# One fit of scales, accumulating x transfers from GpSimd's queue, and a new list of x work in a fused attention and gated feed-forward kernel

## Chip, cores and metric

The kernel runs on one core of one Trainium2 chip. The metric is the device time of one execution in microseconds (us). The kernel before takes 801.61 us, the median of three runs (801.25 to 802.07).

## The reference, cut to what matters

```python
def reference(**kwargs):
    attn_out = _attn_ref(**attn_kwargs)        # [4, 8, 576, 64], softmax attention with a bias of positions
    x = attn_out.transpose(0, 2, 1, 3).reshape(B * S, H * D)      # [2304, 512]
    return _moe_ref(x=x, **moe_kwargs)

def _moe_ref(x, w_gate, w_val, w_out):         # [512, 1536], [512, 1536], [1536, 512]
    gate = 1.0 / (1.0 + np.exp(-(x @ w_gate)))
    val = x @ w_val
    return (gate * val @ w_out).astype(np.float32)
```

The three weight matrices of the feed-forward arrive as float64, the rest as float32; the output is float32. The change lies in the second part, the gated feed-forward.

## The kernel before, in words

**Attention** writes its result to a DRAM tensor `xs`, in which every head has two partial rows (the products with the high and the low part of a split value matrix), and the reciprocals of the softmax sums to `rs`. So a block of x, 128 model columns by 384 tokens, is the sum of two partial blocks of `xs`, times a block of `rs`.

**The feed-forward** (`Moe.run`, line 1162) takes the 2304 tokens as six chunks of 384. Float32 numbers are split into a high and a low part, and each product is three matmuls (high by high, high by low, low by high).

*Chunks 0 and 1* run in 24 steps, numbered 0 to 23, whose order is the string `ORDER` (line 48): a step is one chunk with one of the 12 blocks of 128 hidden columns. In a step TensorE makes the 24 matmuls of gate and value (`gates`, line 890) and then the 9 output matmuls of the step before (`outs`); the last step makes no output matmuls. ScalarE and VectorE apply the sigmoid, the multiply and the split (`gated`, line 905). Beside this the steps convert the float64 weights to float32 blocks, store them to a DRAM tensor `scratch` for later, and take the sum of squares of each block on ScalarE (line 873).

*Chunks 2 to 5* run as two pairs (q = 1: chunks 2 and 3; q = 2: chunks 4 and 5). For a pair, gate (z = 0) and value (z = 1) are 2 by 2 block products with seven multiplications in place of eight (the tables `SUMS`, `VARS` and `PRODUCTS`, lines 71 to 77). Six pairs of hidden blocks by two z by two token pairs make 24 *halves*, `half(h)` (line 1050): even h are z = 0, odd h are z = 1, h = 0 to 11 the first pair, 12 to 23 the second. A half makes seven products of six matmuls in float16 parts, with some output matmuls of the halves before between them; VectorE adds PSUM banks and gates, ScalarE copies banks and applies the sigmoid. In a half, GpSimd makes four sums of weights for the half after the next (line 1036), ScalarE and VectorE make scaled float16 high and low parts of weights for the next half (lines 1042 and 1047), and SyncE's queue loads weights for the third half from here (line 1029).

**The x work of a pair** is a set of small commands, run by `x_do` (line 942), one for each of the blocks B11, B12, B22, B21 (first index: half of the model columns, second index: token chunk) and two slices kc = 0 and 1 of each:

- `l`: load the two partial blocks (`load_x`, line 797: two transfers of 64 partitions) and the reciprocals (`load_r`, two more), all on SyncE's queue;
- `+`: VectorE adds the two partial blocks into a tile `xt` (line 952);
- `*`: VectorE multiplies by the reciprocals (line 954), and ScalarE takes the sum of squares (line 956);
- `T1` to `T4`: VectorE forms the four differences of `SUMS` (line 960);
- `h` and `-`: ScalarE makes the scaled high part (line 966), VectorE the scaled low part (line 968) of each of the seven blocks of `VARS`.

These commands are written out by hand. For the first pair `XTIMES` gives, for each block, the step of `+` and `*` and the step of the load, and `XPLAN` gives the rest by step (the commands are issued at the end of that step; a letter `W` or `S` with a digit loads or sums the weights of half 0, 1 or 2, `h` and `v` with one digit make the parts of half 0's weights, `o` loads output weights). For the second pair `XFILL` is a list with `|` between entries: an entry is taken after each of the seven products of an even half and after the first and third of an odd half, from half 1 on.

**The scales** come from the squares. `fit` reduces squares to a maximum on VectorE, `norm` sums over partitions by a matmul on TensorE that stands in a step after the gates (`NORM`) or in a half after the last product, `read` takes the result out of PSUM, and `fitted` makes the powers of two with small VectorE operations. Before, there are three fits: fit 0 (x of the first pair and the weights of hidden blocks 0 to 7, "A") behind step 18, fit 1 (weights of blocks 8 to 11, "B", and the output weights) behind step 20, and fit 2 (x of the second pair) in half 6. So gate and value have two sets of scales, by hidden block, and `gs` holds two factors for the gating multiply.

**Order.** Each engine and queue runs its instructions in the order in which the program issues them. SyncE's queue holds all loads and stores of this stage; GpSimd has no transfers.

Of the kernel before, what the change touches and what calls it, by code (L numbers as in the profile page):

```python
# [715 lines left out]
class Moe:  # L716
# [212 lines left out]
    def store(self, c, t):  # L929
# [5 lines left out]
        i = 6 + c // 2 - 1  # L935
        self.nc.scalar.activation(out=ob, in_=po, func=AF.Copy, **({"scale": self.ends[:, i:i + 1]} if c > 1 else {}))
# [32 lines left out]

    def xtile(self, q):  # L970
        return self.pools["xt" if q == 1 else "xt2"].tile([128, self.T], F32, tag="xt", name="xt")

    def fit(self, b):

        s = self.squares
        for i, g in enumerate(((s[:, 24:32], s[:, 0:16]), (s[:, 16:24], s[:, 40:52]), (s[:, 32:40],))[b]):
            self.nc.vector.tensor_reduce(out=self.most[:, 2 * b + i:2 * b + i + 1], in_=g, axis=mybir.AxisListType.X, op=ALU.max)  # L980
# [178 lines left out]
    def run(self):  # L1159
# [4 lines left out]
        with ExitStack() as ph, tc.manual_schedule():  # L1164
# [111 lines left out]
```

## Time and profile before

| | us |
|---|---|
| median of three runs (lowest, highest) | 801.61 (801.25, 802.07) |
| the profiled execution, whole | 801.25 |
| its span, first to last instruction | 799.5 |
| TensorE busy in the span | 757.7 |
| VectorE busy | 665.3 |
| ScalarE busy | 572.8 |
| GpSimd busy | 344.7 |

The page names TensorE matmuls PE and weight loads PEld, VectorE DVE, ScalarE ACT, GpSimd POOL and SyncE SP; L952 is line 952 of the kernel. Times in the views are microseconds from the start of the span unless marked ns. The attention part ends at about 370 us; the steps run from 362 to 520 us and the halves from there to the end. Step 18 begins at 481.20, half 0 at 520.28, half 1 at 531.87 and half 12 at 658.25, each read off the first matmul of the step or half.

### The profile page before, as it was taken

To read this page: it belongs to the slowest core of one execution; us is meant where nothing else is said; L and a number is where in the kernel's file an instruction comes from. 1 tells how busy PE (TensorE), PEld (TensorE's weight loads), DVE (VectorE), ACT (ScalarE), POOL (GpSimd) and SP (SyncE) were. 2 spreads that over 40 slices of the span, in tenths; PEclk is the share of its full clock that TensorE was granted. 3 is DMA by queue.
4 is the path that set the end of the run, shared out by engine and by line. 5 is a ranking of instruction groups with operands and counts; after the bars stand their busy time and mean duration, and the time that the engine had idled before them with its cause. 6 is when DMAs were issued, how large, how long until landed. Compare 5 with 4: busy or idle time off the path is not lost.

```text
span 799.5 us, 17532 instructions
## 1 busy us (share of the span) xinstructions
PE 757.7 (95%) x6359; PEld 605.2 (76%) x6359; DVE 665.3 (83%) x1358; ACT 572.8 (72%) x1222; POOL 344.7 (43%) x401
## 2 busy tenths in 40 slices
PE   7999989999999999898999999988999999999997
PEld 4888879999999998887998998854545555555553
DVE  6788888999998999996699899868899986777762
ACT  5888769989989988885666666566656657666653
POOL 1233559999999998960000000114253222533100
PEclk8999999999999999999999999999999999999999
DMA  6543434664664667746887732235442211522102
GB/s 199 153 147 126 124 104 122 176 172 125 181 179 123 179 178 211 206 140 209 299 271 243 228 124 106 93 115 169 149 135 80 80 53 49 163 80 80 54 1 79
DMA packets 66263, 114.00 MB, mean 143 GB/s; under 512 B 7296, under 2 KB 28928, under 8 KB 66176
## 3 DMA queue, kind: packets, MB, share of 16 engines
q1 hardware_dynamic: 64256, 109.93, 45.6%
q10 hardware_dynamic: 1920, 2.95, 1.1%
q8 instruction: 50, 0.82, 0.4%
q14 instruction: 37, 0.30, 0.1%
HBM read 79.75 MB, written 23.67 MB: 129 GB/s over the span
## 4 chain that ended last, share of the span: by engine, by line
PE 57%; DVE 23%; ACT 9%; DMA 5%; issue 4%; SPq 1%; ACTq 0%; DVEq 0%
PE po L924 10%; PE pg L1078 9%; PE sc L565 8%; PE acc L650 7%; PE pu L1078 6%; PE pt L588 6%; PE bps L358 3%; DMA xin<-xs 2%; PE pu L900 2%; PE y L334 2%; DVE btmp L366 2%; PE pg L900 2%; DVE wv L1047 2%; DVE xq L968 2%; DVE en L569 1%
## 5 line engine op out<-in xcount | busy, mean ns | idle before, releaser
L1036 POOL TENSOR_TENSOR ws<-wm 128x256 f32<-128x256 f32 x44 | 41.2, 936 | 303.9 <-DMA wm<-scratch 275.5
L1078 PEld LDWEIGHTS <-wv 128*128 128x128 f16 x1008 | 98.1, 98 | 91.7 <-issue 17.3
L572 ACT ACTIVATE en<-en,mn 128x576 f32<-128x576 f32 x144 | 111.7, 776 | 31.0 <-DVE mn L569 30.0
L1078 PE MATMUL pg<-xq,wv 128*128 128x384 f16 x576 | 109.3, 326 | 9.5 <-ACT c L1104 6.7
L565 PE MATMUL sc<-k,QS 128*128 128x288 f32 x640 | 111.6, 300 | 1.3 <-DVE bias L374 0.6
L569 DVE CUSTOM_DVE_ANT_0 en<-sc,bias 128x576 f32<-128x576 f32 x128 | 93.8, 751 | 7.4 <-PE sc L565 6.4
L565 PEld LDWEIGHTS sc<-k,QS 128*128 128x128 f32 x640 | 91.6, 188 | 2.4 <-PE sc L565 0.8
L588 PE MATMUL pt<-ident,en 128*128 128x128 f32 x576 | 87.1, 274 | 3.7 <-DVE aL L488 1.9
L924 PE MATMUL po<-wo,gh 128*128 128x512 f16 x288 | 85.6, 379 | 0.0
L1078 PE MATMUL pu<-xq,wv 128*128 128x384 f16 x432 | 82.0, 326 | 1.5 <-DVE c L1084 1.2
L650 PE MATMUL acc<-aH,vv 128*128 128x288 f32 x240 | 75.6, 332 | 3.0 <-DVE xe L653 2.8
L1084 DVE TENSOR_TENSOR c<-pu,c 128x384 f32<-128x384 f32 x72 | 40.0, 555 | 41.4 <-PE pu L1078 24.5
L588 PEld LDWEIGHTS pt<-ident,en 128*128 128x128 f32 x576 | 68.4, 141 | 7.2 <-ACT en L572 3.3
L488 DVE TENSOR_TENSOR aL<-pt,aH 128x512 fp32r<-128x512 f32 (+1 forms) x112 | 66.7, 607 | 7.2 <-ACT aH L487 7.2
L358 PE MATMUL bps<-cfs,ind 128*128 128x64 bf16 x1458 | 67.4, 193 | 3.2 <-DVE bias L374 2.4
L339 ACT ACTIVATE ind<-y 128x576 bf16<-128x576 f32 x100 | 62.2, 653 | 10.5 <-PE y L334 8.1
L650 PE MATMUL acc<-aL,vv 128*128 128x288 f32 x240 | 66.6, 294 | 0.0
L1096 ACT ACTIVATE gh<-c 128x384 f16<-128x384 f32 x48 | 25.1, 523 | 57.6 <-DVE c L1094 57.6
L358 PEld LDWEIGHTS <-ind 128*128 128x128 bf16 x1458 | 58.6, 98 | 9.5 <-DVE bias L374 4.2
L492 POOL TENSOR_TENSOR aL<-ar,aH 128x512 fp32r<-128x512 f32 x48 | 62.4, 1300 | 3.9
L487 ACT ACTIVATE aH<-pt 128x512 fp32r<-128x512 f32 (+1 forms) x112 | 57.5, 529 | 0.0
L900 PE MATMUL pg<-xhi,w 128*128 128x384 f32 x192 | 54.2, 340 | 2.2 <-ACT g L909 1.8
(177 smaller groups left out, 1910.3 us busy)
## 6 DMA issues: line engine op xcount, KB each, us to landing
wm<-scratch SPq DMA_DIRECT2D x48, 256.0 KB
kr<-in_k_dram SPq DMA_DIRECT2D x32, 288.0 KB
QS<-part SPq DMA_DIRECT2D x64, 144.0 KB
xs<-xe SPq DMA_DIRECT2D x32, 288.0 KB
xin<-xs SPq DMA_DIRECT2D x48, 192.0 KB
scratch<-wm SPq DMA_DIRECT2D x27, 256.0 KB
wo<-scratch SPq DMA_DIRECT2D x24, 256.0 KB
vr<-in_v_dram SPq DMA_DIRECT2D x16, 320.0 KB
```

The lines of the kernel that those rows point to most:

```text
L339: nc.scalar.activation(out=o, in_=y[:, :, 0:HF], func=AF.Sigmoid, scale=float(2.0 ** 64))
L358: nc.tensor.matmul(out=o, lhsT=st, rhs=cfs[:, part], start=(part == 0), stop=(part == 2))
L488: return lambda: nc.vector.tensor_tensor(out=lo, in0=ps, in1=hi.bitcast(F32), op=ALU.subtract)
L492: nc.gpsimd.tensor_tensor(out=lo, in0=src, in1=hi.bitcast(F32), op=ALU.subtract)
L565: nc.tensor.matmul(out=ps[:, e, 0:HF], lhsT=l, rhs=r[:, HF * e:HF * e + HF], start=(i == 0), stop=(i == len(mms) - 1))
L569: nc.vector.tensor_tensor_reduce(out=half(en), in0=ps[:, :, 0:HF], in1=half(nbias), scale=-0.125, scalar=3.0e38, op0=ALU.add, op1=ALU.min, ...
L572: nc.scalar.activation(out=en, in_=en, func=AF.Exp, bias=mn, scale=-1.0, accum_out=sm)
L588: nc.tensor.transpose(pt[:, J], en[:, 128 * J:128 * J + 128], ident)
L650: nc.tensor.matmul(out=acc[:, 0:HF], lhsT=l, rhs=r, start=(i == 0), stop=(i == len(mms) - 1))
L900: self.nc.tensor.matmul(out=(pg, pu)[z], lhsT=l, rhs=r, start=(kc == 0 and i == 0), stop=(kc == 3 and i == 2))
L924: self.nc.tensor.matmul(out=po, lhsT=l[:, tt], rhs=r, start=(first and i == 0), stop=(last and i == 2))
L1078: nc.tensor.matmul(out=p, lhsT=W[i][:, l, at + kc], rhs=V[b][:, r, kc], start=(new and n == 0), stop=(n == 5), skip_group_check=not new)
```

## The change

- One fit, of the first pair's x, all gate and value weights and the output weights together, stands behind step 19, with its matmul in step 20. The two weight scales become one, `gs` a constant, and `ends` and `tmp` go. The second pair's fit stays, as fit 1.
- `l` now takes the destination tile `xt` at once and loads the first partial block straight into it; `+` is an accumulating transfer of the second partial block into the same tile, issued from GpSimd's queue (two transfers of 64 partitions each). It stands one step after the load in the first pair, and three or more entries after it in most of the second pair's list.
- `XPLAN` is rewritten: T10, T30 and T20 move to steps 9, 11 and 13, the scaled parts to steps 20 to 23.
- `XFILL` is rewritten and begins with half 0.

```diff
 XPLAN = {
-    18: "f0", 19: "g0 W0 W1 T10 T30 hB110 hT10 T20 -B110 -T10 hB210", 20: "T40 hT20 hB220 -B210 -T20 S0 hT30 hT40 -B220 -T30 -T40 f1",
-    21: "T11 T31 hB111 hT11 T21 T41 -B111 -T11 hB211 hT21 h0 h1 -B211 -T21 S1 g1", 22: "hB221 hT31 hT41 -B221 -T31 -T41 v0 v1 h2 h3 v2 v3 W2 o0 o1"}
-NORM = {19: 0, 21: 1}
+    9: "T10", 11: "T30", 13: "T20", 19: "f0 W0 W1 T40 T11 T31", 20: "g0 hB110 hT10 hB210 T21 -B110 -T10 hT20 T41 -B210 S0",
+    21: "hT40 hB220 -T20 h0 hT30 -T40 -B220 h1 -T30 hB111 v0 hT11 S1 -B111",
+    22: "hB211 -T11 v1 hT21 h2 -B211 h3 v2 hT31 -T21 v3 o0 o1", 23: "hT41 hB221 -T31 -T41 -B221 W2"}
+NORM = {20: 0}
-XFILL = ("lB110 lB120|.|.|.|+B110|*B110 lB220|+B120|*B120 lB210|T10|+B220|*B220 lB111|+B210|*B210 lB121|T30|+B111|*B111 lB221|"
-         "+B121|*B121 lB211|T20|+B221|*B221|+B211|*B211|f2|T40|T11|.|g2 hB110|-B110 hT10|-T10 hB220|-B220 hT20|-T20 hB210|"
-         "-B210 hT30|-T30 hT40|-T40 hB111|-B111 hT11|T31 -T11|T21 hB221|-B221 hT21|T41 -T21|hB211 -B211|hT31 -T31|hT41 -T41")
+XFILL = ("lB110|.|.|+B110 lB120|.|.|+B120|*B110 lB220|*B120 lB210|+B220|T10 +B210|.|*B220 lB111|.|*B210 lB121|T30 +B111|"
+         "T20 +B121|*B111 lB221|*B121 lB211|+B221|T40 +B211|.|T11|.|*B221|*B211|T31|f1|T21|.|T41|.|.|.|g1 hB110 hT10|-B110 hB210|"
+         "-T10 hT20|.|-B210 hT40|-T20 hT30|.|-T40 hB220|.|-T30 hB111|-B220 hT11|-B111 hB211|.|-T11 hT21|-B211 hT31|.|-T21 hT41|.|"
+         "-T31 hB221|-T41 -B221")
...
         if what == "l":
             c, k = 2 * q + (n[2] == "2"), kc + 2 * (n[1] == "2")
-            t[n, "in"], t[n, "rec"] = self.load_x(c, k), self.load_r(c, k)
+            t[n] = self.xtile(q)
+            self.load_half(nc.sync, t[n], c, k, 0)
+            t[n, "rec"] = self.load_r(c, k)
         elif what == "+":
-            t[n], i = self.xtile(q), t.pop((n, "in"))
-            nc.vector.tensor_tensor(out=t[n], in0=i[:, 0], in1=i[:, 1], op=ALU.add)
+            c, k = 2 * q + (n[2] == "2"), kc + 2 * (n[1] == "2")
+            self.load_half(nc.gpsimd, t[n], c, k, 1, accum_op=ALU.add)
...
+    def load_half(self, eng, t, c, k, s, **how):
+        for e in range(2):
+            r = 256 * k + 128 * e + 64 * s
+            eng.dma_start(out=t[64 * e:64 * e + 64], in_=self.xs[r:r + 64, self.T * c:self.T * c + self.T], **how)
+
     def xtile(self, q):
-        return self.pools["xt" if q == 1 else "xt2"].tile([128, self.T], F32, tag="xt", name="xt")
+        return self.pools["xt" if q == 1 and "xt2" not in self.pools else "xt2"].tile([128, self.T], F32, tag="xt", name="xt")
...
-        for i, g in enumerate(((s[:, 24:32], s[:, 0:16]), (s[:, 16:24], s[:, 40:52]), (s[:, 32:40],))[b]):
-            self.nc.vector.tensor_reduce(out=self.most[:, 2 * b + i:2 * b + i + 1], in_=g, axis=mybir.AxisListType.X, op=ALU.max)
+        for i, g in enumerate(((s[:, 24:32], s[:, 0:24], s[:, 40:52]), (s[:, 32:40],))[b]):
+            self.nc.vector.tensor_reduce(out=self.most[:, 3 * b + i:3 * b + i + 1], in_=g, axis=mybir.AxisListType.X, op=ALU.max)
...
-        t = [self.tmp[:, i:i + 1] for i in range(2)]
-        if b == 1:
-            v.tensor_tensor(out=t[0], in0=self.ups[:, 1:2], in1=self.ups[:, 2:3], op=ALU.min)
-            v.tensor_scalar(out=self.gs, in0=self.uns[:, 1:3], scalar1=t[0], scalar2=float(2.0 ** -12), op0=ALU.mult, op1=ALU.mult)
-            v.tensor_tensor(out=t[1], in0=u[1], in1=u[2], op=ALU.max)
-            v.tensor_scalar(out=t[1], in0=t[1], scalar1=u[3], scalar2=float(2.0 ** 12), op0=ALU.mult, op1=ALU.mult)
-        if b:
-            v.tensor_tensor(out=self.ends[:, 5 + b:6 + b], in0=t[1], in1=u[0 if b == 1 else 4], op=ALU.mult)
+        x, w, o, both, last = (self.uns[:, i:i + 1] for i in (3 * b, 1, 2, 4 + 2 * b, 5 + 2 * b))
+        v.tensor_tensor(out=both, in0=x, in1=w, op=ALU.mult)
+        v.tensor_scalar(out=last, in0=both, scalar1=o, scalar2=float(2.0 ** 12), op0=ALU.mult, op1=ALU.mult)
+        self.un[b + 1] = both, last
...
-            nc.vector.scalar_tensor_tensor(out=g, in0=src, scalar=self.gs[:, int(k > 3):int(k > 3) + 1], in1=g, op0=ALU.mult, op1=ALU.mult)
+            nc.vector.scalar_tensor_tensor(out=g, in0=src, scalar=float(2.0 ** -12), in1=g, op0=ALU.mult, op1=ALU.mult)
...
-                    todo += [f"{w}{XFIRST[n % 4]}{n // 4}" for w, at in (("+", add), ("*", add), ("l", load)) if at == i]
+                    todo += [f"{w}{XFIRST[n % 4]}{n // 4}" for w, at in (("+", load + 1), ("*", add), ("l", load)) if at == i]
...
-                if h == 1:
+                if h == 0:
                     self.fill = XFILL.split("|")
```

## Rows read from the trace of the kernel before

**Rows 1.** The page, part 1: busy us of each engine, share, instructions.
```profile
PE 757.7 (95%) x6359; PEld 605.2 (76%) x6359; DVE 665.3 (83%) x1358; ACT 572.8 (72%) x1222; POOL 344.7 (43%) x401
```

**Rows 2.** Windows: steps 18-23, halves 1-11, 12-19; length, busy us, clock, DMA share, GB/s.
```profile
481.20:520.28 39.08, 36.71 (x191) 33.77 (x192) 35.36 (x85) 22.81 (x48) 2.92 (x4) 1.00 0.29 101
...
531.87:658.25 126.38, 117.34 (x646) 63.16 (x646) 112.11 (x182) 80.22 (x162) 46.42 (x48) 1.00 0.39 119
658.25:743.93 85.68, 85.68 (x481) 46.96 (x480) 65.21 (x97) 54.43 (x102) 29.38 (x32) 1.00 0.28 92
```

**Rows 3.** Timeline of PE: start, us, instruction, [idle before and what ended it].
```profile
481.20 0.44 PE L900 MATMUL pg<-xhi,w 128*128 128x384 f32 x1 [0.43 <-ACT g L909]
...
505.30 0.16 PE L987 MATMUL pu<-most,ones 128*128 128x2 bf16 x1 [0.58 <-DVE most L980]
...
516.82 0.45 PE L900 MATMUL pu<-xhi,w 128*128 128x384 f32 x1 [0.72 <-DVE g L910]
...
520.28 0.49 PE L1078 MATMUL pg<-xq,wv 128*128 128x384 f16 x2 [1.07 <-ACT g L909]
...
551.18 1.14 PE L1078 MATMUL pg<-xq,wv 128*128 128x384 f16 x6 [1.78 <-ACT c L1104]
```

**Rows 4.** Waits from 520 to 660: us in total, times, longest us.
```profile
ACT room L956 <- DVE xt L954: 7.7, 7, 2.0
PE pg L1078 <- ACT c L1104: 6.7, 9, 1.8
```

**Rows 5.** The chain that ended last, around 551 us: start, us, what.
```profile
546.88 0.38 DVE xt L952
...
549.10 1.01 DVE xt L954
...
550.13 0.62 ACT room L956 x2
550.75 0.39 ACT c L1104
```

**Rows 6.** Groups by line and form on DVE, 395 to 490: busy us, mean ns | idle.
```profile
L863 DVE TENSOR_TENSOR w<-wm,w 128x512 fp32r<-128x512 f32 x24 | 16.4, 683 | 0.0
...
L206 DVE TENSOR_SCALAR wm<-wm 128x512 f32<-128x512 f32 x24 | 10.1, 419 | 0.0
...
L952 DVE TENSOR_TENSOR xt<-xin 128x384 f32<-128x384 f32 x8 | 4.4, 550 | 0.0
```

**Rows 7.** The same in halves 1 to 11, 531.87 to 658.25.
```profile
L968 DVE SCALAR_TENSOR_TENSOR xq<-xt,ups,xq 128x384 f16<-128x384 f32 x14 | 10.4, 744 | 1.6 <-ACT xq L966 1.6
...
L952 DVE TENSOR_TENSOR xt<-xin 128x384 f32<-128x384 f32 x8 | 6.0, 749 | 0.0
L954 DVE TENSOR_TENSOR xt<-xt,xrec 128x384 f32<-128x384 f32 x8 | 6.0, 745 | 0.0
L960 DVE TENSOR_TENSOR xt<-xt 128x384 f32<-128x384 f32 x8 | 5.4, 681 | 0.0
```

**Rows 8.** One line's instructions, L803: ns min/median/max, first and last start us.
```profile
L803 SPq DMA_DIRECT2D xin<-xs x48: 599/606/1386, 294.4 to 578.1; - x48
```

**Rows 9.** The same for L1036, GpSimd's weight sums.
```profile
L1036 POOL TENSOR_TENSOR ws<-wm x44: 722/997/1178, 512.8 to 747.9; 128x256 f32<-128x256 f32 x44
```

**Rows 10.** Timeline of POOL: its first instruction after the attention part.
```profile
512.76 0.77 POOL L1036 TENSOR_TENSOR ws<-wm 128x256 f32<-128x256 f32 x1 [151.13 <-DMA wm<-scratch]
```

**Rows 11.** The chain that ended last: two x loads, from issue to landing.
```profile
416.54 6.21 DMA xin<-xs
...
467.44 3.01 DMA xin<-xs
```

**Rows 12.** Timeline of DVE: the last multiply of the steps, and the second fit.
```profile
485.43 0.56 DVE L954 TENSOR_TENSOR xt<-xt,xrec 128x384 f32<-128x384 f32 x1
...
512.78 0.16 DVE L1000 TENSOR_SCALAR norms<-norms 128x2 int32<-128x2 int32 x1
...
516.21 0.56 DVE L910 TENSOR_TENSOR g<-pu,g 128x384 f32<-128x384 f32 x1
```

More of the change, by code (lines that the diff above doesn't have):

```diff
@@ L934, in store @@
             ob = self.pools["ob"].tile([128, DM], F32, name="ob")
-        i = 6 + c // 2 - 1
-        self.nc.scalar.activation(out=ob, in_=po, func=AF.Copy, **({"scale": self.ends[:, i:i + 1]} if c > 1 else {}))
+        self.nc.scalar.activation(out=ob, in_=po, func=AF.Copy, **({"scale": self.un[c // 2][1]} if c > 1 else {}))
         self.nc.sync.dma_start(out=self.out[self.T * c + 128 * t:self.T * c + 128 * t + 128, :], in_=ob)
@@ L982, in norm @@
     def norm(self, b):
-        n = 2 if b < 2 else 1
-        self.sums = self.spare[:, 0:n]
-        self.nc.tensor.matmul(out=self.sums, lhsT=self.ones, rhs=self.most[:, 2 * b:2 * b + n], start=True, stop=True, skip_group_check=True)
+        a = slice(3 * b, 3 if b == 0 else 4)
+        self.sums = self.spare[:, 0:a.stop - a.start]
+        self.nc.tensor.matmul(out=self.sums, lhsT=self.ones, rhs=self.most[:, a], start=True, stop=True, skip_group_check=True)
     def read(self, b):
-        n = 2 if b < 2 else 1
@@ L991, in read @@
-        self.nc.vector.tensor_scalar(out=self.norms[:, 2 * b:2 * b + n], in0=self.sums, scalar1=float(2.0 ** -100), scalar2=None, op0=ALU.max)
+        self.nc.vector.tensor_scalar(
+            out=self.norms[:, 3 * b:3 if b == 0 else 4], in0=self.sums, scalar1=float(2.0 ** -100), scalar2=None, op0=ALU.max)
     def fitted(self, b):
-        v, n = self.nc.vector, 2 if b < 2 else 1
-        m, up, un = (t[:, 2 * b:2 * b + n].bitcast(I32) for t in (self.norms, self.ups, self.uns))
+        v, a = self.nc.vector, slice(3 * b, 3 if b == 0 else 4)
@@ L1000, in fitted @@
+        m, up, un = (t[:, a].bitcast(I32) for t in (self.norms, self.ups, self.uns))
         v.tensor_scalar(out=m, in0=m, scalar1=1, scalar2=None, op0=ALU.logical_shift_right)
@@ L1041, in high @@
             self.wv.setdefault((k, z), []).append(w)
-            nc.scalar.activation(out=w[:, 0, 0:t[i].shape[1]], in_=t[i], func=AF.Copy, scale=self.up["AB"[k > 3]])
+            nc.scalar.activation(out=w[:, 0, 0:t[i].shape[1]], in_=t[i], func=AF.Copy, scale=self.up["w"])
         def low(i):
@@ L1046, in low @@
             n = s.shape[1]
-            nc.vector.scalar_tensor_tensor(out=w[:, 1, 0:n], in0=s, scalar=self.up["AB"[k > 3]], in1=w[:, 0, 0:n], op0=ALU.mult, op1=ALU.subtract)
+            nc.vector.scalar_tensor_tensor(out=w[:, 1, 0:n], in0=s, scalar=self.up["w"], in1=w[:, 0, 0:n], op0=ALU.mult, op1=ALU.subtract)
         return load, sums, [lambda i=i: high(i) for i in range(4)], [lambda i=i: low(i) for i in range(4)]
@@ L1058, in half @@
         q, k, z = 1 + h // NF, h % NF // 2, h % 2
-        W, V, un = self.wv.pop((k, z)), self.var[q], self.un[q, int(k > 3)]
+        W, V, un = self.wv.pop((k, z)), self.var[q], self.un[q][0]
         c = 2 * q
@@ L1152, in load_wo @@
         t = self.pools["wfirst"].tile([128, 2, 4, 128], F32, tag="w", name="wo")
-        w, m, s = t[:, 0].rearrange("p k f -> p (k f)").bitcast(F16).rearrange("p (s k f) -> p s k f", s=2, k=4), t[:, 1], self.ups[:, 3:4]
+        w, m, s = t[:, 0].rearrange("p k f -> p (k f)").bitcast(F16).rearrange("p (s k f) -> p s k f", s=2, k=4), t[:, 1], self.up["o"]
         self.wos[f] = w, [
@@ L1174, in run @@
             self.squares, self.room = keep("squares", 52), keep("room", 256)
-            self.norms, self.ups, self.uns, self.ends = (keep(n, 8) for n in ("norms", "ups", "uns", "ends"))
-            self.gs, self.tmp = keep("gs", 2), keep("tmp", 2)
+            self.norms, self.ups, self.uns = (keep(n, 8) for n in ("norms", "ups", "uns"))
             self.most, self.ones = (self.pools["fit"].tile([128, w], BF16, name=n) for n, w in (("most", 6), ("ones", 128)))
             nc.gpsimd.memset(self.ones, 1.0)
-            self.up = {1: self.ups[:, 0:1], "A": self.ups[:, 1:2], "B": self.ups[:, 2:3], 2: self.ups[:, 4:5]}
+            self.up = {n: self.ups[:, i:i + 1] for i, n in enumerate((1, "w", "o", 2))}
             self.un, self.fits = {}, []
```

5 lines of the change are left out of this document (removed).

## The prediction

> **What bounds the kernel now.** I read the page's busy shares first: TensorE works 95% of the span, VectorE 83%, GpSimd 43% [rows 1]. An average over stages says little, so next come the windows. In the last quarter shown TensorE never idles while VectorE is busy 65.21 of 85.68 us; in halves 1 to 11 TensorE is busy 117.34 of 126.38 us and VectorE 112.11; in steps 18 to 23 it is 36.71 of 39.08 and 35.36 [rows 2]. So 9.04 us and 2.37 us of TensorE time are lost exactly where the x work of the two pairs lies on VectorE. The clock is 1.00 in all three, so it is left out of what follows.
>
> The TensorE timeline then gives the gaps one by one: 0.43 us at 481.20, and 0.58, 0.72 and 1.07 us, which are the whole 2.37 of steps 18 to 23; the longest of the halves is 1.78 us at 551.18 [rows 3]. The waits show who ends them in the halves: a copy of a PSUM bank on ScalarE; and ScalarE's squares wait 7.7 us for VectorE's multiply of x [rows 4]. The chain around 551 us puts the two together: the add of the two partial x rows, the multiply, the square that ScalarE meets in its queue, and only then the copy that frees the bank [rows 5]. That is the pattern to keep in mind: one x operation on VectorE, late, blocks ScalarE's next copy, and TensorE after it.
>
> **The change part by part.** *The adds of partial rows leave VectorE.* Sixteen adds (line 952) go: eight of 550 ns in steps 6 to 17 [rows 6], eight of 749 ns in the halves, 6.0 us [rows 7]. In the halves I put all 6.0 us on the path, since VectorE is what ends the gaps there: -6.0 (between 0, if the gaps are another engine's, and -9.04, all idle). In the steps the adds of steps 8, 10 and 12 are replaced by the differences T10, T30 and T20, moved to steps 9, 11 and 13, operations of the same size, so they are neutral; those of steps 14 to 17 have no replacement. What that frees closes the gap of 0.43 us at 481.20, which lies behind a multiply and its square: -0.4 (0 to -0.43).
>
> *What the adds become.* Each is now two accumulating transfers of 96 KB from GpSimd's queue, 32 in all, while SyncE issues the same four transfers per row block as before, with half the x bytes. The trace has no transfer on GpSimd's queue. For the issue the nearest rows bound it: 0.61 us (SyncE's x load) to 1.18 us (GpSimd's longest sum) [rows 8, 9]; with four sums of some 1.0 us a half and otherwise idle, GpSimd takes two to four more issues a half beside them. In steps 4 to 16 it stands idle (its wait of 151.13 us) [rows 10]. So the issue costs nothing while GpSimd's sums keep ahead of their users, half a half later; gone, that cover would cost what the sums are late. For the landing, an x load takes 3.01 to 6.21 us [rows 11]; load and accumulation come one after another, so 6.0 to 12.4 us for both. I take 6 to 9, since the DMA share in the halves is 0.39 [rows 2] and the 3.01 is from the quieter stretch. In the steps the shortest cover is that of the last block: issued at 467.44, multiplied at 485.43 [rows 11, 12], 18 us. In the halves a product with its share of output matmuls takes 85.68 / 8 / 7 = 1.53 us [rows 2]; the written plan leaves 6 such slots between load and multiply for two blocks (9.2 us), 7 for two (10.7), 9 or more for four. Within 9 us all is covered: 0. Behind a multiply that waits stand, on VectorE, the sums of banks and the gating, so a late landing would go straight to TensorE.
>
> The destination tile is now taken at the load. The block loaded at step 15 is the eleventh of ten x tiles, but B12 of the first slice is dead after T30 in step 11, so SyncE finds one free: 0.
>
> *One fit.* The second fit's operations, from 512.78 until the gating at 516.21, 3.4 us with small operations stretched to 0.6, go [rows 12], and with them the norm matmul that waited 0.58 us. The 0.72 gap waits for the gating multiply directly behind that fit, and the 1.07 for ScalarE's sigmoid, whose queue was held by scalings that follow it [rows 3]. The remaining fit gets one reduction more and must wait for the squares of the last weights, one step later than before; its scalings of x come a step later too. VectorE's load in steps 19 to 23 falls by the 3.4 us and by three differences of 0.55 moved ahead, 5.1 us, which outweighs the later start. The last gap remains in part, as ScalarE must read the bank after the last gates: I leave 0.4. So -2.0 (0, if the later start eats it, to -2.4). The constant factor in the gating and the scale of the outputs are the same instructions: 0. W2's load slips from step 22 to 23, behind two output-weight loads on SyncE; half 0 covers it: 0.
>
> *The second pair spread anew.* The even halves 2, 4, 6, 8, 10 carry 5, 7, 5, 7 and 6 x operations on VectorE now; with the adds gone they would carry 3, 4, 4, 7 and 6, and in the new list 4, 4, 2, 4 and 4. Evening out the last: -0.8, a choice between 0 and the -3.0 of idle that is left after the adds. Against it, half 1 gets two multiplies where it had loads only, and it has gaps already: +1.5, twice 0.745 [rows 7], between 0 and 2.7 (with their squares, 0.62 each [rows 5]).
>
> **Sum.** -6.0 - 0.4 - 2.0 - 0.8 + 1.5 = -7.7 against the profiled execution's 801.25, so 793.55; the median of the runs stands 0.36 above that execution, so I say **793.9**.
>
> The nearest rule against this change is in the Trainium skill, "SBUF — State Buffer", section "Summary: rules for kernel authors": a transfer issued from GpSimd starves while VectorE runs in a mode that takes both ports, so it should come from another queue. Rows fit the existence of such a mode: a one-input operation takes 419 ns where a two-input one of equal width takes 683 [rows 6]. By the rule the transfers of the steps would be late by some of those 0.42 us, far under the 18 us of cover, while in the halves the four x groups are all two-input operations [rows 7]; no run here shows a starved transfer yet. "DMA: Bandwidth & Descriptors", section "Anatomy of one DMA", prices a transfer from GpSimd at about 2.0 us plus its bytes at 436 GB/s: an estimate of 2.2 us, by which the first rival below would hardly occur.
>
> **The rivals.** *The sums land late* (slower). Place: the multiplies of halves 1 to 5. With L us from load to landed sum the price is 2 x (L - 9.2) + 2 x (L - 10.7); it eats the 7.7 from L = 11.9 on, and at the bound of 12.4 it is 9.8: 803.7. For it: loads took 6.21 us where the queues were full. Against it: the share of 0.39. 0.10. If starvation of GpSimd's queue is real, this is how it would show.
>
> *VectorE is not what holds the halves.* The gaps are counted on ScalarE's bank copies [rows 4], and if these are late of themselves, the adds' absence only makes VectorE idle: the steps' -2.4 and half 1's +1.5 remain, which is 801.6 - 0.9 = 800.7. Against it: VectorE is 89% busy there and the one long gap runs through it. 0.12.
>
> *Every gap closes.* 0.43 + 2.37 + 9.04 = 11.84 off: 789.8. For it: the late halves, with VectorE at 76%, have no gap at all. Against it: 106 us of VectorE work for eleven halves is still about 90% of 117. 0.16.
>
> *The transfers change nothing by themselves.* Should GpSimd's issues disturb VectorE as its sums do (749 ns in the halves against 550 in the steps for the same add [rows 6, 7]), sixteen pairs could give back half of the 6.0: about 797; this lies inside the forecast's range.
>
> **How the numbers follow.** 0.2% of 801.6 is 1.6 us, about what a measurement of this kernel can tell from no change. The forecast, with its neighbourhood from 791 to 799.5, has 0.62; closing all 0.16; the halves unmoved 0.12, mostly inside 0.2%; late sums 0.10. Faster: 0.62 + 0.16 + 0.04 = 0.82; same 0.08; slower 0.10. The range reaches from 789 (every gap closed and a little of matmul refill) to 800.5, leaving out the late sums and part of the two outer cases.
>
> **What would show it.** Right: no line-952 add; 32 transfers on GpSimd's queue; VectorE never idle before a multiply for a transfer; no gap at a norm matmul in step 21 and none of 0.72 behind it; halves begin some 2.5 us earlier; TensorE's idle time in halves 1 to 11 near 4 to 5 us, with half 1 longer than before. Wrong: multiplies that wait for GpSimd's transfers; GpSimd's sums late for the weights of the next half; the same 9 us of gaps with VectorE idle before them.

## The result, and the profile after

The changed kernel takes **794.71 us**, the median of four runs (793.62 to 795.15), against 801.84 us (801.25 to 802.98) for the kernel before on the same chip: a ratio of 0.9907, 95% interval 0.9890 to 0.9925. The forecast was 793.9 us. A second measurement of the changed kernel, among the experiments below, gave 795.37 us and 0.9897 (0.9876 to 0.9918). The profiled execution took 795.05 us, with a span of 793.3 us at a granted clock of 0.995.

The page after: busy times by engine (part 1), a row of the queues (part 3) and a row of the groups (part 5).

```profile
PE 757.6 (96%) x6358; PEld 605.3 (76%) x6358; DVE 654.3 (82%) x1329; ACT 573.2 (72%) x1222; POOL 373.7 (47%) x433
...
q0 software_dynamic: 2560, 3.15, 2.8%
...
L976 POOL DMA_DIRECT2D xt<-xs x32 | 26.7, 1041 | 106.6 <-DMA xt<-xs 94.4
```

The issues of transfers, in the view of the DMA (last column: median us from issue to landing), and the spread of the landings, in the view of their line.

```profile
xt<-xs POOLq DMA_DIRECT2D x32, 96.0 KB, 4.3
...
DMA to landing us min/median/max: 2.9/4.3/8.0
```

Against [rows 1], TensorE does the same work, VectorE has 11.0 us less and GpSimd 29.0 us more. Most of GpSimd's part are the 32 issues, 1.04 us each in the mean and, as they overlap in part, 26.7 us together. It stands idle 94.4 us in front of them until SyncE's half of the same block has landed.

The windows answer to [rows 2], with the same columns: steps 18 to 23, half 0, halves 1 to 11, half 1 alone, halves 12 to 19.

```profile
478.62:515.73 37.11, 37.11 (x197) 34.44 (x196) 29.90 (x66) 22.13 (x48) 2.53 (x3) 1.00 0.38 128
515.73:529.23 13.50, 11.01 (x58) 6.67 (x58) 10.47 (x18) 8.83 (x18) 4.66 (x6) 1.00 0.26 50
529.23:651.78 122.55, 117.44 (x647) 63.75 (x647) 108.13 (x172) 80.47 (x162) 56.18 (x60) 0.99 0.41 113
529.23:541.23 12.00, 8.75 (x45) 4.80 (x45) 9.42 (x14) 7.11 (x16) 7.29 (x8) 0.92 0.65 172
651.78:737.46 85.68, 85.68 (x482) 46.96 (x481) 63.92 (x97) 54.50 (x102) 30.49 (x32) 1.00 0.29 93
```

(The first window opens inside step 17, 1.4 us ahead of step 18.) TensorE has no idle time left in the steps shown, where it had 2.37 us; in halves 1 to 11 it idles 122.55 - 117.44 = 5.11 us, where it had 9.04. The later halves are what they were, 85.68 us. But half 0 is new on the list: 13.50 us with 2.5 us idle, where the timeline of before has it from 520.28 to 531.87, 11.59 us; and half 1 takes 12.00, against 9.90, at a granted clock of 0.92.

TensorE's timeline, its longest gaps now (start, us, what, then the idle time before and what ended it).

```profile
519.11 1.14 PE L1077 MATMUL pu<-xq,wv 128*128 128x384 f16 x6 [1.52 <-DVE g L912]
...
529.24 1.14 PE L1077 MATMUL pg<-xq,wv 128*128 128x384 f16 x6 [0.79 <-ACT c L1090]
...
538.39 1.14 PE L1077 MATMUL pg<-xq,wv 128*128 128x384 f16 x6 [2.56 <-ACT c L1103]
539.36 2.09 PE L1077 MATMUL pu<-xq,wv 128*128 128x384 f16 x6
541.24 1.91 PE L1077 MATMUL pg<-xq,wv 128*128 128x384 f16 x6
```

The four gaps of the steps in [rows 3] are gone. In their place stands the 1.52 in half 0, which waits for the last gating multiply. VectorE's timeline shows why that is late.

```profile
511.11 0.61 DVE L971 SCALAR_TENSOR_TENSOR xq<-xt,ups,xq 128x384 f16<-128x384 f32 x1
...
513.26 1.10 DVE L971 SCALAR_TENSOR_TENSOR xq<-xt,ups,xq 128x384 f16<-128x384 f32 x1
514.29 1.23 DVE L1046 SCALAR_TENSOR_TENSOR wv<-ws,ups,wv 128x512 f16<-128x512 f32 x1
515.43 1.09 DVE L971 SCALAR_TENSOR_TENSOR xq<-xt,ups,xq 128x384 f16<-128x384 f32 x1
516.45 1.21 DVE L1046 SCALAR_TENSOR_TENSOR wv<-ws,ups,wv 128x512 f16<-128x512 f32 x1
517.58 0.60 DVE L971 SCALAR_TENSOR_TENSOR xq<-xt,ups,xq 128x384 f16<-128x384 f32 x1
518.11 0.47 DVE L1046 SCALAR_TENSOR_TENSOR wv<-wm,ups,wv 128x256 f16<-128x256 f32 x1
518.51 0.55 DVE L912 TENSOR_TENSOR g<-pu,g 128x384 f32<-128x384 f32 x1
```

With one fit the scaled parts come later and crowd in front of that multiply. And the low parts of x, 0.61 us at 511.11 and 0.60 at 517.58, take 1.09 to 1.10 between 513.1 and 517.1, where GpSimd makes its sums, as its timeline has it:

```profile
513.12 0.83 POOL L1035 TENSOR_TENSOR ws<-wm 128x256 f32<-128x256 f32 x1 [41.32 <-ACT gh L913]
...
516.07 1.04 POOL L1035 TENSOR_TENSOR ws<-wm,ws 128x256 f32<-128x256 f32 x1
517.05 3.33 POOL L976 DMA_DIRECT2D xt<-xs  x4
```

The gap of 2.56 has a second price. Behind it the same six matmuls take 2.09 and 1.91 us in place of 1.14. The windows of that place, the columns as above, show why:

```profile
538.39:539.36 0.97, 0.97 (x7) 0.58 (x7) 0.94 (x2) 0.00 (x0) 0.97 (x2) 1.00 0.80 160
539.36:541.24 1.88, 1.88 (x7) 0.84 (x6) 1.49 (x4) 1.05 (x2) 0.39 (x1) 0.51 0.67 117
541.24:542.99 1.75, 1.75 (x8) 0.83 (x7) 1.47 (x3) 0.32 (x1) 0.00 (x0) 0.55 1.03 288
```

After TensorE had stood still for 2.56 us and run one group at full speed, the granted clock fell to 0.51 and 0.55, the lower of its two levels (1.2 of 2.4 GHz), and was back at 1.00 by 543. TensorE is busy 8.75 us in half 1 and 10.99 in half 2, where the same matmuls took 8.02 and 10.22 before, at a clock of 1.00: the fall costs 0.73 + 0.77 = 1.5 us. (Read off the starts, where 1.88 and 1.75 us stand in place of 0.97 each, it is 1.7.)

The waits between 520 and 660 us (us in total, times, longest) answer to [rows 4].

```profile
PE pg L1077 <- ACT c L1103: 5.1, 6, 2.6
ACT room L959 <- issue: 4.5, 3, 1.7
...
ACT room L959 <- DVE xt L957: 1.1, 1, 1.1
```

No row of VectorE names a transfer of x. TensorE's waits for bank copies fell from 6.7 to 5.1 us, and half of what is left is the one of 2.56 in half 1. It comes about as in [rows 5] (VectorE and ScalarE in the timeline):

```profile
535.79 1.07 DVE L957 TENSOR_TENSOR xt<-xt,xrec 128x384 f32<-128x384 f32 x1
...
536.95 0.52 ACT L959 ACTIVATE room<-xt 128x384 bf16<-128x384 f32 x1 [1.70 <-issue]
...
537.87 0.47 ACT L1103 ACTIVATE c<-pg 128x384 f32<-128x384 f32 x1
```

The square starts when the multiply has ended, at 536.86 (its wait reads as "issue", also in the row above), and the bank copy that TensorE waits for stands behind it.

### The profile page after: what moved, and what is told of

The parts are those of the page before. It is cut to its first block, busy times and chain, and to the rows that moved or that the text cites. A ratio compares the mean times of both kernels' runs of the same rounds, so it can differ in the third digit from the quotient of the medians.

```text
span 793.3 us, 17584 instructions
## 1 busy us (share of the span) xinstructions
PE 757.6 (96%) x6358; PEld 605.3 (76%) x6358; DVE 654.3 (82%) x1329; ACT 573.2 (72%) x1222; POOL 373.7 (47%) x433
## 5 line engine op out<-in xcount | busy, mean ns | idle before, releaser
L1035 POOL TENSOR_TENSOR ws<-wm 128x256 f32<-128x256 f32 x44 | 44.5, 1011 | 161.5 <-DMA wm<-scratch 90.6
L976 POOL DMA_DIRECT2D xt<-xs x32 | 26.7, 1041 | 106.6 <-DMA xt<-xs 94.4
```

## The experiments

The table sets all kernels side by side, in us. Stages are read off the first matmul of a step or half in the timeline of each profiled execution; "all" runs from the first matmul of step 0 to the last matmul of the kernel. Halves 12 to 23 take 136.45 in every one of them and are left out. Each row of stages is thus one execution: for e1 and e3 the fastest of the runs, for e4, e7, e8 and e12 the slowest. In these executions the clock falls in half 1, as in the changed kernel, in e8, e4 and e7, and in no other kernel in any half. What lies ahead of step 0 (362.24 us before, 362.70 after) is untouched by the change but moves by some 2 us from one execution to another, so stages are compared rather than spans. Ratios are to runs of the kernel before on the same chip, with 95% intervals.

| kernel | steps 9-17 | 18-23 | halves 0-1 | 2-11 | all | median | ratio |
|---|---|---|---|---|---|---|---|
| before | 58.95 | 39.08 | 21.49 | 116.48 | 432.46 | 801.84 | 1 |
| after | 57.49 | 35.67 | 25.51 | 110.54 | 425.53 | 794.71 | 0.9907 (0.9890-0.9925) |
| e8 after again | 57.48 | 35.66 | 25.85 | 110.44 | 426.07 | 795.37 | 0.9897 (0.9876-0.9918) |
| e1 adds back | 58.95 | 35.76 | 24.07 | 113.51 | 428.62 | 800.09 | 0.9971 (0.9955-0.9988) |
| e2 fits back | 57.78 | 37.58 | 23.46 | 110.44 | 425.87 | 796.97 | 0.9933 (0.9920-0.9947) |
| e3 spread back | 57.51 | 35.66 | 23.07 | 115.59 | 427.98 | 797.87 | 0.9950 (0.9936-0.9963) |
| e9 transfers alone | 57.85 | 37.59 | 22.16 | 115.45 | 429.62 | 801.63 | 0.9983 (0.9970-0.9996) |
| e4 no cover | 57.47 | 35.66 | 26.13 | 116.53 | 432.09 | 800.70 | 0.9979 (0.9967-0.9991) |
| e5 gate first | 57.46 | 35.66 | 23.97 | 110.73 | 424.04 | 795.06 | 0.9901 (0.9883-0.9919) |
| e6 half 1 free | 57.47 | 35.66 | 23.13 | 114.22 | 426.66 | 796.92 | 0.9926 (0.9907-0.9946) |
| e7 early W2 | 57.48 | 37.27 | 24.55 | 111.45 | 428.07 | 795.46 | 0.9912 (0.9893-0.9931) |
| e10 square later | 57.46 | 35.66 | 23.74 | 109.82 | 422.99 | 791.91 | 0.9863 (0.9850-0.9876) |
| e11 square and gate | 57.49 | 35.66 | 23.41 | 109.54 | 422.39 | 792.28 | 0.9867 (0.9842-0.9891) |
| e12 mix | 57.49 | 35.66 | 22.77 | 111.18 | 423.46 | 793.51 | 0.9879 (0.9853-0.9904) |

**One part undone at a time.** Diffs are against the changed kernel. First the adds return to VectorE.

```diff
...
-            self.load_half(nc.gpsimd, t[n], c, k, 1, accum_op=ALU.add)
+            t[n], i = self.xtile(q), t.pop((n, "in"))
+            nc.vector.tensor_tensor(out=t[n], in0=i[:, 0], in1=i[:, 1], op=ALU.add)
...
```

> The kernel after, with one part undone: the partial x rows are loaded together again and added on VectorE (at the places of the lists where the accumulating transfers stand for the second pair, together with the multiply for the first). Fit, step list and fill list stay as after. Theory A (the adds' removal carries the halves): 799 to 801, 5 to 6 us slower than after, with TensorE idle again some 5 us more in halves 1 to 11 and 1.5 us more in steps 10 to 19. Rival B (the lists and the fit carry the gain): at most 796.5, VectorE's adds fitting in beside.

Measured: 800.09 us, some 5 us of the gain gone, inside theory A's range. In the profile it is 3.1 us: the whole 1.46 of steps 9 to 17, as A has it, and 2.97 in halves 2 to 11, with 1.5 less in half 1; TensorE idles 2.3 us more in halves 1 to 11 (7.4 against 5.11), not 5. Half 0 keeps its gap of 1.5 us without any transfer there, so that gap is not the transfers'.

Then the fits, their scales and the plan of the steps of before, with the transfers and the new list kept.

```diff
...
-NORM = {20: 0}
+NORM = {19: 0, 21: 1}
...
```

> The kernel after, with the two fits and two weight scales of before and the step list of before; accumulating transfers and the new fill list stay. Theory A: the 3.2 us that steps 21 to 23 gained come back as gaps (0.58 at the norm matmul, 0.7 behind the second fit, 1 at the first half), but half 0, which got 1.9 us longer after, gets shorter by most of that, because the scaled parts are then earlier: 795 to 797 in all. Rival C (the one fit is worth what steps 21 to 23 gained, half 0's loss is of another origin): 797.5 to 798.5. Rival D (the fit is worth nothing): 794 to 795.

Measured: 796.97 us, inside A's numbers. The stages say how: steps 18 to 23 lose 1.9 us and half 0 wins back 1.8 (11.71 against 13.50). So **one fit moves idle time from the steps to half 0**; in the profiled executions it is worth 0.3 us, in the timed runs 2 to 3. Part of that difference may be the clock, which does not fall in this execution: half 1 has two gaps, of 1.63 and 2.05 us.

Then the second pair's list with its operations at their old places, taken from half 1 on as before (the list itself is not shown), with each pair of transfers two or three entries ahead of its multiply.

```diff
...
-                if h == 0:
+                if h == 1:
```

> The kernel after, with the fill list in the order and at the places of before (from half 1 on, no multiply before half 2), each accumulating transfer put two to three entries ahead of its multiply. Theory A (the new spread is worth little, its two multiplies in half 1 cost 2 us and the evening of the later halves gives back as much): 793.5 to 796. Rival B (the spread carries the halves' gain): 797 to 799, with 3 us or more of gaps back in halves 4, 6 and 8.

Measured: 797.87 us, inside theory B's range, but not at B's places: halves 4, 6 and 8 idle 2.3 us, against 0.45 in the changed kernel. Halves 2 to 11 take 5.05 us more, halves 0 and 1 take 2.4 less. One multiply met the shorter cover and waited (VectorE's timeline):

```profile
573.52 0.56 DVE L955 TENSOR_TENSOR xt<-xt,xrec 128x384 f32<-128x384 f32 x1 [2.67 <-issue]
```

Its transfers landed at 573.44. TensorE's longest gap follows from that wait, 2.36 us in half 5, where the changed kernel idles 0.42: so some 2 of the 5.05 us are the late transfer's, and this run alone does not give the list's worth.

**The transfers alone**, put into the kernel before (the diff is against that): loads and accumulation as in the change, with the old fits and places.

```diff
...
-            nc.vector.tensor_tensor(out=t[n], in0=i[:, 0], in1=i[:, 1], op=ALU.add)
+            c, k = 2 * q + (n[2] == "2"), kc + 2 * (n[1] == "2")
+            self.load_half(nc.gpsimd, t[n], c, k, 1, accum_op=ALU.add)
...
```

> The kernel before with one part of the change alone: the accumulating transfers from GpSimd's queue in place of VectorE's adds. Two fits, step list and the places of all other entries of the fill list are those of before (from half 1 on); each transfer of the second pair stands one or two entries behind its load. Theory A (the adds' removal is the largest part, and fit and spread add little to it): 795 to 797.5, 4.5 to 6.5 us faster than before. Theory J (the parts only work together, since each alone leaves another wait in half 0, 1 or 6): 797.5 to 800. Rival B (fit and lists carry all): above 800.5.

Measured: 801.63 us beside 803.12 for the kernel before in that job, 1.4 us off; J, which it misses by a little, is the nearest. The stages give 2.8: 1.1 in steps 9 to 17, 1.5 in steps 18 to 23, and only 1.0 in halves 2 to 11, where all eight adds of that pair had gone; halves 0 and 1 lose 0.7 again. Half 6 shows what became of them. Before, VectorE's add stood beside GpSimd's sums (VectorE, ScalarE and TensorE in the timeline):

```profile
592.97 1.08 DVE L952 TENSOR_TENSOR xt<-xin 128x384 f32<-128x384 f32 x1
...
595.11 0.55 DVE L954 TENSOR_TENSOR xt<-xt,xrec 128x384 f32<-128x384 f32 x1
...
597.79 0.97 PE L1078 MATMUL pg<-xq,wv 128*128 128x384 f16 x5 [1.20 <-ACT c L1104]
```

With the transfers alone, the same place:

```profile
592.61 1.18 POOL L1042 TENSOR_TENSOR ws<-wm 128x256 f32<-128x256 f32 x1
...
593.12 1.08 DVE L955 TENSOR_TENSOR xt<-xt,xrec 128x384 f32<-128x384 f32 x1
...
594.28 0.52 ACT L957 ACTIVATE room<-xt 128x384 bf16<-128x384 f32 x1 [1.36 <-issue]
...
595.20 0.71 ACT L1161 ACTIVATE wo<-wo,ups 128x512 f16<-128x512 f32 x1
...
595.81 0.47 ACT L1110 ACTIVATE c<-pg 128x384 f32<-128x384 f32 x1
...
596.33 0.97 PE L1084 MATMUL pg<-xq,wv 128*128 128x384 f16 x5 [1.54 <-ACT c L1110]
```

The multiply moved into the add's slow place and took its 1.08 us; the square waited for it 1.36 us on ScalarE, two scalings followed, and only then came the bank copy for which TensorE waits. The gap grew from 1.20 to 1.54. Halves 8 to 11, which hold no add (the last ran at 592.97), keep their gaps: 2.36 us of idle before, 2.56 here. In the changed kernel this place of half 6 has no multiply, and the half falls from 12.51 to 10.09 us.

**How much cover the transfers need.** In the changed list each pair of the second token pair's transfers stands two or three entries behind its load and two to five ahead of its multiply. Here it stands one entry ahead.

```diff
-XFILL = ("lB110|.|.|+B110 lB120|.|.|+B120|*B110 lB220|*B120 lB210|+B220|T10 +B210|.|*B220 lB111|.|*B210 lB121|T30 +B111|"
-         "T20 +B121|*B111 lB221|*B121 lB211|+B221|T40 +B211|.|T11|.|*B221|*B211|T31|f1|"
+XFILL = ("lB110|.|.|lB120|.|.|+B110|*B110 lB220 +B120|*B120 lB210|.|T10|+B220|*B220 lB111|+B210|*B210 lB121|T30|"
+         "T20 +B111|*B111 lB221 +B121|*B121 lB211|.|T40|.|T11|+B221|*B221 +B211|*B211|T31|f1|"
...
```

> The kernel after, with each accumulating transfer of the second pair put in the entry right before its multiply, nothing else changed. The two transfers take some 2 us to issue and 4.3 us to land, an entry is 1.5 us. Theory A (the cover by the list is needed): each of the eight multiplies waits 3 to 5 us and VectorE passes most of it on: 805 to 825. Rival E (GpSimd runs ahead of the program's places, so the list's distance matters little): under 798.

Measured: 800.70 us, between the two theories. Three of the eight multiplies waited. Two of them in VectorE's timeline (an awaited transfer reads as "issue"; each starts 0.08 us after its transfers landed):

```profile
557.62 0.56 DVE L955 TENSOR_TENSOR xt<-xt,xrec 128x384 f32<-128x384 f32 x1 [4.75 <-issue]
...
583.17 0.84 DVE L955 TENSOR_TENSOR xt<-xt,xrec 128x384 f32<-128x384 f32 x1 [0.85 <-issue]
```

The third waited 1.2 us. The other five did not wait, because GpSimd issues ahead of the list's places where its queue lets it, as in rival E: the first multiply's transfers went out 11.9 us ahead of it (518.78 to 530.68). The first wait made half 3 16.80 us long, with 4.80 of idle, against 11.76. So late sums do cost TensorE their wait, as the rival *late sums* of the prediction had it. The list as changed leaves enough room, but not much: there the closest sum landed 0.8 us ahead of its multiply.

**Half 0 and half 1.** The last two gating parts one step later, so that they don't queue with the scaled parts:

```diff
-    22: "hB211 -T11 v1 hT21 h2 -B211 h3 v2 hT31 -T21 v3 o0 o1", 23: "hT41 hB221 -T31 -T41 -B221 W2"}
+    22: "hB211 -T11 v1 hT21 h2 -B211 h3 hT31 -T21 o0 o1", 23: "hT41 hB221 v2 -T31 v3 -T41 -B221 W2"}
```

> The kernel after, with the low parts of half 0's third and fourth weights moved on VectorE from step 22 to step 23, behind the last step's gating. Theory F (half 0's gap of 1.52 us at 519.1 is VectorE coming late to the last gating multiply, behind four low parts that run at twice their length beside GpSimd's sums): that gap shrinks to 0.3 or less and the kernel gains 1.0 to 1.5 us on after. Rival G (VectorE as a whole is late there, and the moved parts are missed elsewhere in half 0): the gap goes and comes back within half 0, 0 to 0.4 us.

Measured: 795.06 us, no gain that shows, as in rival G. The gap of 1.52 became three of about 0.5, and half 0 takes 13.50 as before. In the profiled execution the gap in half 1 was 1.21 us and the clock stayed up, so "all" is 1.5 us shorter; the timed runs don't show it.

No multiply in half 1, the list closed up behind it:

```diff
-XFILL = ("lB110|.|.|+B110 lB120|.|.|+B120|*B110 lB220|*B120 lB210|+B220|T10 +B210|.|*B220 lB111|.|*B210 lB121|T30 +B111|"
+XFILL = ("lB110|.|.|+B110 lB120|.|.|+B120|.|.|*B110 lB220|.|*B120 lB210|+B220|T10|+B210|.|*B220 lB111|*B210 lB121|T30 +B111|"
...
```

> The kernel after, with the fill list written so that half 1 has no multiply: the first two stand in half 2, and what follows is shifted and closed up (the second pair's fit one half later). Theory H (the 2.1 us that half 1 got longer are its two multiplies and their squares in front of a bank copy): half 1 falls from 12.0 to about 10 us and the later halves take back at most half: 1 to 2 us faster than after. Rival I (half 1 is held by GpSimd's sums beside it, whatever is in the list): half 1 stays at 11.5 to 12, no gain.

Measured: 796.92 us. Half 1 falls to 9.64, as theory H has it, so its two multiplies cost 2.4 us, 0.7 of it by the clock; but halves 2 to 11, where the same work is denser, take 3.7 more and not at most half of what half 1 gave.

W2's load in step 20 in place of 23:

```diff
-    9: "T10", 11: "T30", 13: "T20", 19: "f0 W0 W1 T40 T11 T31", 20: "g0 hB110 hT10 hB210 T21 -B110 -T10 hT20 T41 -B210 S0",
+    9: "T10", 11: "T30", 13: "T20", 19: "f0 W0 W1 T40 T11 T31", 20: "g0 W2 hB110 hT10 hB210 T21 -B110 -T10 hT20 T41 -B210 S0",
...
-    22: "hB211 -T11 v1 hT21 h2 -B211 h3 v2 hT31 -T21 v3 o0 o1", 23: "hT41 hB221 -T31 -T41 -B221 W2"}
+    22: "hB211 -T11 v1 hT21 h2 -B211 h3 v2 hT31 -T21 v3 o0 o1", 23: "hT41 hB221 -T31 -T41 -B221"}
```

> The kernel after, with the load of half 2's weights in step 20 in place of step 23, so that GpSimd's first sums run some steps earlier. Theory F2 (the collision of these sums with VectorE's low parts of step 22 makes half 0's first gap): the sums run before 510, the low parts take 0.6 us in place of 1.1, the gap of 1.52 shrinks by 1 us, 0.7 to 1.2 us faster. Rival G: no difference, because the sums only collide with other operations, or because no tile is free earlier.

Measured: 795.46 us, no gain. Half 0 is back at 11.60: GpSimd's sums now start at 498.97, and the low parts in front of the gating take their short times again (VectorE's timeline):

```profile
516.08 0.61 DVE L971 SCALAR_TENSOR_TENSOR xq<-xt,ups,xq 128x384 f16<-128x384 f32 x1
516.61 0.75 DVE L1046 SCALAR_TENSOR_TENSOR wv<-ws,ups,wv 128x512 f16<-128x512 f32 x1
```

But the sums now meet VectorE around step 21, where it is busy 6.12 us against 5.56, and steps 22 and 23 take 1.6 us more. The collision only moved. (The clock also fell for longer in this execution, to a mean of 0.81 in half 1 and 0.92 in half 2.)

**ScalarE's order.** [Rows 5] had the square of x in front of the bank copy. Here the squares of the second pair are issued one list entry later:

```diff
-            nc.scalar.activation(out=self.room[:, 0:T // 2].bitcast(BF16), in_=t[n], func=AF.Square, accum_out=self.squares[:, i:i + 1])
+            square = lambda x=t[n]: nc.scalar.activation(
+                out=self.room[:, 0:T // 2].bitcast(BF16), in_=x, func=AF.Square, accum_out=self.squares[:, i:i + 1])
+            if q == 2:
+                self.owed.append(square)
+            else:
+                square()
...
+                owed, self.owed = self.owed, []
+                for f in owed:
+                    f()
                 for w in self.fill.pop(0).split():
```

> The kernel after, with the second pair's squares issued on ScalarE one list entry (one or more products) behind their multiply in place of right behind it; nothing else changed. Theory K (in halves 1 to 5 TensorE's gaps come through ScalarE: a square that waits for VectorE's late multiply stands before the copy that frees a bank): the gap of 2.56 us in half 1 falls to 1 or less, halves 1 to 3 get 1.5 to 2.5 us shorter, the kernel 1 to 2.5 us faster than after. Rival L (the copy waits for the bank's own product and VectorE's sums anyway): the gaps stay within 0.5 us in sum.

Measured: **791.91 us** (791.33 to 792.47), ratio 0.9863 (0.9850 to 0.9876): about 3 us under the changed kernel, theory K and a little more. The interval lies below that of the changed kernel's first measurement and touches that of its second (0.9876 to 0.9918). The row that answers to the waits, and then the multiply, the copy and the gap that was 2.56 us:

```profile
PE pg L1082 <- ACT c L1108: 2.4, 5, 0.8
```

```profile
535.12 1.08 DVE L957 TENSOR_TENSOR xt<-xt,xrec 128x384 f32<-128x384 f32 x1
...
535.84 0.48 ACT L1108 ACTIVATE c<-pg 128x384 f32<-128x384 f32 x1
...
536.37 1.14 PE L1082 MATMUL pg<-xq,wv 128*128 128x384 f16 x6 [0.75 <-ACT c L1108]
...
537.85 1.14 PE L1082 MATMUL pu<-xq,wv 128*128 128x384 f16 x6 [0.34 <-DVE c L1088]
```

VectorE's multiply at that place takes 1.08 us as it did; only the copy no longer stands behind a square that waits for it, and starts before the multiply has ended. With the gap the fall of the clock is gone too. Halves 1 and 2 get 3.4 us shorter (1.5 of clock, 1.9 of idle time), and halves 3 to 11 give 1.0 back. This beats both kernels. Two variants on top of it: with e5's gating, and with one multiply moved out of half 1 besides:

```diff
-XFILL = ("lB110|.|.|+B110 lB120|.|.|+B120|*B110 lB220|*B120 lB210|+B220|T10 +B210|.|*B220 lB111|.|*B210 lB121|T30 +B111|"
+XFILL = ("lB110|.|.|+B110 lB120|.|.|+B120|*B110 lB220|+B220|*B120 lB210|T10|+B210|*B220 lB111|+B111|.|*B210 lB121|"
...
```

> The kernel after with the squares one entry later (as in e10) and half 0's third and fourth low parts behind the last gating (as in e5). Theory M (half 0's gap before its second product only moved in e5 and came back as three of 0.5 us, so VectorE's total there decides): the same as e10, within 0.5 us. Rival F (with the squares out of the way the gap stays closed): 1 to 1.5 us faster than e10, 0.985 of the kernel before or less.

> As e11, and the fill list with one multiply moved from half 1 to half 2 and what follows closed up, so that half 4 has five x operations on VectorE in place of four; the transfers stand at least three entries ahead of their multiplies. Theory N (a half holds up to four such operations in an even and two in an odd half without a gap, and half 1, which has fewer output matmuls to hide behind, one): half 1 falls by 0.7 us or more, half 4 grows by at most 0.3, 0.5 us faster than e11. Rival O (as in e6, what is moved out of half 1 is missed later): the same or slower.

They take 792.28 and 793.51 us: the same, as in theory M, and the same or a little slower, as in rival O (half 1 did not fall in e12: 10.15 us, against 9.91 in e11). The changed kernel itself, run again beside e5 and e7:

> The changed kernel once more, as it is, on the same chip as these three, for the comparison with them: 0.9907 of the kernel before, within 0.2%.

Its stages repeat within 0.1 us but for halves 0 and 1, which came out 0.3 us longer.

## Why the prediction was right, and where it was not

The total was right, -7.7 against a measured -7.1 (794.71 - 801.84), and the side and the signs in the profile too: no add on VectorE, 32 transfers from GpSimd, no multiply that waits, no gap at a norm matmul, half 1 longer, and 5.11 us of idle time in halves 1 to 11 where 4 to 5 were said. One sign was off: half 0 begins 4.5 us earlier, at 515.74, where 2.5 were said, and gives 1.9 of them back. So the total is in part luck, as the terms of the sum were wrong in ways that cancelled.

- *Adds of the halves, -6.0, all on the path.* The step that failed. Alone they bring 1.0 us in halves 2 to 11 (e9), as the last part put in 3.0 (e1). The prediction set the busy time of the adds against the idle time of halves 1 to 11 as one sum, without asking whether the two lie in the same halves: the adds stand in halves 2 to 6, and 2.36 us of the gaps lie in halves 8 to 11. And where both met, in half 6, the next operation fell into the add's slow place.
- *Evening of the even halves, -0.8.* Mis-sized the other way: with transfers in, the new list takes 5.0 us off halves 2 to 11 (115.45 to 110.44 from e9 to e2; from e3 to after it is as much, with the late transfer of e3 in it). *Two multiplies in half 1, +1.5*: 2.4 by e6, of which 1.7 goes with the square's place alone (e10: 12.00 to 10.27).
- *The clock, left out of the sum because it was 1.00.* In the profiled execution it falls behind the new gap in half 1, between 539.4 and 543: 1.5 us that no term had.
- *One fit, -2.0.* Steps 18 to 23 gained 3.4; the transfers alone give 1.5 there and the fit 1.9 on top (e9, e2), or the fit 3.3 without them (e1). Half 0 gave 1.9 back. The prediction named this as its bound of 0 ("if the later start eats it") and set it aside, as VectorE has less to do in the steps; it left out that the low parts are pushed beside GpSimd's sums, where they take 1.1 us in place of 0.6, ahead of the last gating multiply. Net about 0.3 in the profiles. A part of the gain in the steps is no wait at all: a step in which TensorE never idles, step 9 for one, takes 6.31 us before, in e2 and in e9, and 6.27 in every kernel with the one fit. Nothing on record says why.
- *Adds of the steps, -0.4.* The gap of 0.43 us closed as said. The operations at steps 8 to 13 were called neutral, but step 10 has 0.77 us of idle where it had 1.26, and about the same with the transfers alone, which bring 1.1 us in steps 9 to 17.
- *Transfers at nothing.* No multiply waited, but not for the reason given. An issue takes 1.04 us, inside the bounds taken (0.61 to 1.18). From the issue of a block's load to the landed sum, though, the second pair's blocks took 10.2 to 16.2 us and not 6 to 9; six of the eight took more than the 11.9 at which *late sums* was to eat the whole gain. They were in time because SyncE issued the loads 13.6 to 24.5 us ahead of the multiplies, where the slots of the list had given 9.2 or more. Two errors cancelled, and the closest sum landed only 0.8 us ahead of its multiply (576.00 and 576.78); what shorter cover does is shown by e3 and e4.

The rivals: *late sums* did not occur, but were real at less cover. *VectorE not what holds the halves* was half true: the gaps follow the list, and ScalarE's own order is worth about 3 us (e10). *Every gap closes* did not occur. *Transfers that disturb VectorE*: the multiply's mean rose from 745 ns [rows 7] to 964 in halves 1 to 11. Beside issues alone nothing shows it: in the changed kernel, from step 19 to half 11, sixteen VectorE operations on two SBUF inputs ran there, and all kept their time (the multiply at 551.90: 0.55 us). But where one of GpSimd's sums follows an issue directly, an operation takes longer than beside sums alone (GpSimd and VectorE in the timeline after):

```profile
557.16 1.64 POOL L976 DMA_DIRECT2D xt<-xs  x2 [5.03 <-DMA xt<-xs]
558.34 1.21 POOL L1035 TENSOR_TENSOR ws<-wm 128x256 f32<-128x256 f32 x1
...
558.23 1.75 DVE L957 TENSOR_TENSOR xt<-xt,xrec 128x384 f32<-128x384 f32 x1
```

Operations of this kind, 1.40 to 2.00 us long, occur in every profiled execution with transfers from GpSimd, and in neither of the two without (before and e1). So this rival was real in a place or two of each kernel, for some 0.3 to 0.8 us of VectorE's time each. What that costs TensorE is not shown by itself.

Of the rules weighed, the one of the Trainium skill, "SBUF — State Buffer", section "Summary: rules for kernel authors", that a transfer issued by GpSimd starves beside VectorE's two-port mode, has no clear sign in these traces: 2.9 to 8.0 us from issue to landing, where SyncE's x loads took 3.01 and 6.21 [rows 11], and no wait where the cover is that of the list. No run here tests it by itself. The estimate of 2.2 us by the Trainium skill, "DMA: Bandwidth & Descriptors", section "Anatomy of one DMA", was too low against the median of 4.3.

**The parts depend on each other.** By the column "all", the transfers alone give 2.8 us, fit and list together 3.8 (e1), transfers and fit 4.5 (e3), transfers and list 6.6 (e2), the three 6.9. The last part put in is worth 3.1 (transfers), 2.5 (list) or 0.3 (fit), each with the 1.5 us of the clock against it, as the clock falls in no half of the profiled e1, e2 and e3.

Open: in the timed runs e1, e2 and e3 lie 5, 2 and 3 us above the changed kernel, in the profiles 3.1, 0.3 and 2.5. The mean granted clock of each run bears on that. The profiled e1 (797.69 us) had 0.996; of its nine other runs one had 0.996 too (798.47 us), and eight had 0.991 to 0.993 and took 799.68 to 802.30. In e8 the runs at 0.992 took 795.35 to 796.14 us, those at 0.995 to 0.997 took 792.96 to 795.39. So the clock costs some runs more than the profiled ones show, e1's above all; where in the kernel it fell in them is not on record. The runs of one kernel spread over 1 to 5 us, so the size of each part is known to about 2 us only. Of half 0's idle time, 2.5 us, no version took more than a part without giving it back elsewhere.

## What to carry to other kernels

Before a removed operation is credited, put it and the idle time that it is to close on one axis, stage by stage: an engine's busy time in a stage with gaps is not the gaps' cause, and the next operation in order may inherit the bad place. Look then at the queue of the engine that releases the bound one: an instruction there that waits for a late result (here a square on ScalarE) and that nobody needs soon is moved behind the copy that is needed, which here was worth 3 us for no work saved. Partial sums can be left to accumulating transfers from an idle queue, if they get the room: here 2.9 to 8.0 us from issue to landing, and 10.2 to 16.2 us from the issue of the load on, as the accumulation is issued only after the load has landed and stands behind GpSimd's own work.

## What was not expected of the hardware

VectorE operations on two inputs from SBUF take about 0.5 us longer while GpSimd makes its 128x256 sums: the same low part 0.60 and 1.10 us, the multiply 0.55 and 1.08, the 128x512 low part 0.75 and 1.23. Operations with one of the two inputs in PSUM do not: the ten bank sums that ran beside them from step 19 to half 11 of the changed kernel took 0.54 to 0.56 us. Where a sum directly follows an issue of a transfer it can be more: 1.75 us for the multiply at 558.23. The prediction had seen the means differ (550 and 749 ns) and not that it is a matter of place: where GpSimd's sums stand decides which VectorE operation pays (e7, e9).

A single gap can cost more than its length: behind the 2.56 us in half 1 the clock fell and took 1.5 us more. It also fell at gaps of 2.21 us (e8) and 2.57 us (e4, e7) at that place, in e7 before the gap had ended, and not at 2.05 us there (e2) or 3.69 us in half 3 of e4. What decides is not settled by these runs.
